# Casting and splitting the value product straight from PSUM in a memory-attention and SwiGLU kernel

## The chip, the cores and the metric

The kernel runs on one core of one Trainium2 chip. The metric is the device time of one execution in microseconds (us), lower is better. Five engines work side by side, each through its own queue in order: TensorE (PE; its weight loads are listed as PEld), VectorE (DVE), ScalarE (ACT), GpSimd (POOL) and SyncE (SP, which issues the DMAs here).

## The reference

Eight batches, eight heads, 576 tokens, head width 64 and 32 memory slots per head; then a SwiGLU block of width 1536 on 4608 rows of 512:

```python
a = softmax(phi, axis=tokens)                    # per head: 576 x 32
k_m = einsum('bhsm,bhsd->bhmd', a, k)            # 32 x 64
v_m = einsum('bhsm,bhsd->bhmd', a, v)
attn = softmax(q @ k_m.T / 8, axis=memory)       # 576 x 32
x = (attn @ v_m), heads side by side             # 4608 x 512
xn = x / sqrt(mean(x * x) + 1e-6) * rms_g
out = (silu(xn @ w_gate) * (xn @ w_val)) @ w_out
```

The weights come as float64, and are converted to float32 on the chip.

## The kernel before, in words

Since `x = attn @ v_m`, the product `xn @ w_gate` equals `attn @ (v_m @ w_gate)` with a scale per row. The kernel never forms `x` for it: it multiplies the small `v_m` of a batch with the weights once (the value product, `vp`), and then multiplies the attention with the result. To keep float32 accuracy, each operand of a product is split into a high part, rounded to the type fp32r, and a low part, what the rounding left; a product is then three matmuls (high x high, high x low, low x high).

A first part, up to about 150 us, makes `k_m`, `v_m` and the attention of the first two pairs of batches. Then comes the part that the change touches: 48 units. A unit `i` belongs to a pair of batches `pr` and a block `j` of 128 columns of the hidden layer; 24 units do the first two pairs of batches over the twelve blocks, 24 more do the other two pairs. A unit consists of these steps:

- `vw_steps(i)`: twelve matmuls (line 852) of the split `v_m` (`vm`) with the split weights (`wh`, `wl`) into `vp`, a PSUM tile of 128 x 1024 float32, two banks, with a single buffer. Its step `evac` (lines 858 to 868) empties it: ScalarE copies the lower 64 partitions into a float32 tile `xf` (line 861), and the upper 64 in two copies that swap the two blocks `b` (line 863); ScalarE casts `xf` to the high part `xh` (line 866); GpSimd subtracts to get the low part `xl` (line 867). `xf` has one buffer, `xh` and `xl` have two each.
- `gv_steps(i)`: in two groups of rows and for both `b`, twelve matmuls (line 889) of `xh`, `xl` with the split attention (`ath`, `atl`) into `pg` and `pv` (two PSUM buffers each); ScalarE takes the silu of `pg` into `sg` (line 897), VectorE multiplies it with `pv` into `hf` (line 898); ScalarE casts `hf` to `hh` (line 911), GpSimd subtracts to get `hl` (line 912).
- `out_steps(i)`, at every second unit: for nine tiles of rows, six matmuls (line 931) of `hh`, `hl` with the split output weights into `po` (two PSUM buffers), and VectorE adds `po` to the sum `acc` in SBUF (line 938; line 936 is the first, a copy). After the last block the sums go out by DMA.

During the first 24 units, VectorE also converts the weights of the coming blocks (`convert`, lines 345 to 385: integer operations on the tiles `ex` and `mi`, then `w`; ScalarE takes a step at line 376), ScalarE casts them (line 402), GpSimd subtracts their low part (`wl` and `ol`, line 403), and the split weights are stored to HBM and read back by the second 24 units. Attention of the last two pairs of batches (`attend_steps`, `x2`: lines 977 to 1021, with tiles `S`, `qT`, `rp`, `at`, which share `po`'s PSUM buffers) is spread over these units too.

The order of the work is written out: each step has a due time, counted in units (`VW`, `GV`, `O`, `PRE` and others in a table `PRM`), the steps are issued in that order, and a scheduler then puts each engine's queue in an order by when it reckons things ready. Every step of the lists `vw_steps(i + 1)` and `gv_steps(i)` is placed so that the value product of the next unit is made while the present one is multiplied.

Of the kernel before, what the change touches and what calls it, by code (L numbers as in the profile page):

```python
# [8 lines left out]
F32 = mybir.dt.float32  # L9
# [4 lines left out]
ALU = mybir.AluOpType  # L14
# [77 lines left out]
def kernel(  # L92
# [24 lines left out]
    nc = tc.nc  # L117
    P = 128
# [309 lines left out]
    with ExitStack() as c1:  # L428
        sb = c1.enter_context(tc.tile_pool(name="sb1", bufs=2, reuse_waits="tile"))
# [394 lines left out]
    sb = ctx.enter_context(tc.tile_pool(name="sb2", bufs=1, reuse_waits="tile"))  # L824
# [5 lines left out]
    def where(i):  # L830

        ps_, r = divmod(i, NU * G * 2)
        u, r = divmod(r, G * 2)
        pi, f = divmod(r, 2)
        return ps_, u, ps_ * G + pi, 2 * u + f

    def vw_steps(i):

        ps_, u, pr, j = where(i)

        def mm(cc):
            def f():
                if cc == 0:
                    vw[i] = [ps.tile([P, 2, 2, 256], F32, tag="vw", name=f"vp{i}", bufs=1)]
                vp = vw[i][0]
                vh, vl = vm[pr][:, 0], vm[pr][:, 1]
                wh, wl = (x.rearrange("p hp g f -> p hp (g f)") for x in wsplit[ps_ * NJ + j])
                for e in range(2):
                    def lhs(vt):
                        return vt[:, cc, e].rearrange("p o x -> p (o x)")  # L850
                    for n, (l, r) in enumerate(((vh, wh), (vh, wl), (vl, wh))):
                        nc.tensor.matmul(  # L852
                            vp[:, cc, e, :], lhs(l), r[:, 2 * cc + e, :],
                            start=(n == 0), stop=(n == 2),
                        )
            return f

        def evac():
            vp = vw[i][0]
            xf = sb.tile([P, 2, 2, 256], F32, tag="xf", name=f"xf{i}")  # L860
            nc.scalar.copy(xf[0:64], vp[0:64])
            for b in range(2):
                nc.scalar.copy(xf[64:128, :, b, :], vp[64:128, :, 1 - b, :])  # L863
            xh = sb.tile([P, 2, 2, 256], F32R, tag="xh", name=f"xh{i}", bufs=2)
            xl = sb.tile([P, 2, 2, 256], F32R, tag="xl", name=f"xl{i}", bufs=2)
            nc.scalar.copy(xh, xf)  # L866
            nc.gpsimd.tensor_tensor(out=xl, in0=xf, in1=xh.bitcast(F32), op=ALU.subtract)  # L867
            vw[i] = xh, xl
        return [mm(0), mm(1), evac]

# [248 lines left out]
```

## Time and profile before

| | |
|---|---|
| median of 3 runs | 942.52 us (942.49 to 943.4) |
| the profiled execution | 941.95 us, of which 940.2 us are the span from the first to the last instruction |
| busy in the span: TensorE | 852.0 us (91%) |
| VectorE | 560.4 us (60%) |
| ScalarE | 433.2 us (46%) |
| GpSimd | 408.7 us (43%) |
| mean granted TensorE clock | 0.962 |
| chain of work that ended last | TensorE 69%, VectorE 20%, DMA 3%, ScalarE 3%, GpSimd 1% |

How to read the rows. A row of a group shows the line of the kernel, the engine, the operation, what it writes and reads, partitions x elements and type, and how many there are; behind the first bar stands the busy time in us and the mean duration of one in ns, behind the second how long the engine stood idle just before such instructions, and what ended that. A row of a single line or tile gives the minimum, median and maximum duration in ns. A row of the waits gives who waited for whom: us in total, times, the longest in us. A row in the order of time gives the start and the duration in us, the instruction, how many were merged, and in square brackets the idle time before it with what ended it. Times count from the first instruction. In the slices of the page each digit is the busy share of a fortieth of the span, in tenths. An engine's idle time is no cost in itself: what counts is the chain of work that ends last.

### The profile page before, as it was taken

To read this page: it belongs to the slowest core of one execution; us is meant where nothing else is said; L and a number is where in the kernel's file an instruction comes from. 1 tells how busy PE (TensorE), PEld (TensorE's weight loads), DVE (VectorE), ACT (ScalarE), POOL (GpSimd) and SP (SyncE) were. 2 spreads that over 40 slices of the span, in tenths; PEclk is the share of its full clock that TensorE was granted. 3 is DMA by queue.
4 is the path that set the end of the run, shared out by engine and by line. 5 is a ranking of instruction groups with operands and counts; after the bars stand their busy time and mean duration, and the time that the engine had idled before them with its cause. 6 is when DMAs were issued, how large, how long until landed. Compare 5 with 4: busy or idle time off the path is not lost.

```text
span 940.2 us, 15899 instructions
## 1 busy us (share of the span) xinstructions
PE 852.0 (91%) x6207; PEld 756.7 (80%) x6207; DVE 560.4 (60%) x998; ACT 433.2 (46%) x743; POOL 408.7 (43%) x290
## 2 busy tenths in 40 slices
PE   5799676689889899897799999999999999999998
PEld 4678565679779688786699898798989999999996
DVE  5487969895897976969843463643333333333333
ACT  2566333656547546465454354343343443443430
POOL 2365636562653554454344354253333423433421
PEclk9889877899899999999899999999999999999999
DMA  8997644452343623434223215341202212030046
GB/s 282 254 288 237 225 134 131 143 159 66 98 158 83 187 76 83 161 100 152 90 64 102 68 60 134 85 115 45 90 1 69 67 36 100 1 129 7 1 107 140
DMA packets 85667, 106.42 MB, mean 113 GB/s; under 512 B 38996, under 2 KB 56920, under 8 KB 85592
## 3 DMA queue, kind: packets, MB, share of 16 engines
q1 hardware_dynamic: 85592, 105.41, 37.7%
q8 instruction: 49, 0.80, 0.4%
q14 instruction: 26, 0.21, 0.1%
HBM read 73.93 MB, written 31.46 MB: 112 GB/s over the span
## 4 chain that ended last, share of the span: by engine, by line
PE 69%; DVE 20%; DMA 3%; issue 3%; ACT 3%; POOL 1%; SPq 0%; DVEq 0%; ACTq 0%; POOLq 0%
PE po L931 28%; PE pv L889 13%; PE pg L889 13%; PE vp L852 5%; DVE mi L369 3%; DVE mi L365 3%; DVE w L385 2%; PE kvp L583 2%; PE xp L235 2%; DVE ex L345 2%; DMA phi<-in_phi_dram 2%; DVE ex L358 1%; DVE acc L938 1%; DVE ex L357 1%; DVE ex L352 1%
## 5 line engine op out<-in xcount | busy, mean ns | idle before, releaser
L912 POOL TENSOR_TENSOR hl<-hf,hh 128x512 fp32r<-128x512 f32 (+1 forms) x96 | 143.6, 1496 | 235.1 <-ACT hh L911 180.6
L938 DVE TENSOR_TENSOR acc<-po,acc 128x512 f32<-128x512 f32 x180 | 123.8, 689 | 165.4 <-PE po L931 165.2
L931 PE MATMUL po<-oh,hh 128*128 128x512 f32 x432 | 174.4, 405 | 14.3 <-DVE acc L938 12.0
L867 POOL TENSOR_TENSOR xl<-xf,xh 128x1024 fp32r<-128x1024 f32 x48 | 118.3, 2465 | 137.4 <-ACT xh L866 73.6
L931 PE MATMUL po<-oh,hl 128*128 128x512 f32 x432 | 172.0, 398 | 0.0
L931 PE MATMUL po<-ol,hh 128*128 128x512 f32 x432 | 171.5, 397 | 0.0
L897 ACT ACTIVATE sg<-pg 128x256 f32<-128x256 f32 x192 | 78.5, 411 | 189.3 <-PE pg L889 175.5
L898 DVE TENSOR_TENSOR hf<-pv,sg 128x256 f32<-128x256 f32 x192 | 85.4, 452 | 106.9 <-PE pv L889 65.2
L931 PEld LDWEIGHTS po<-oh,hh 128*128 128x128 f32 x432 | 81.7, 190 | 30.5 <-DVE acc L938 15.3
L889 PE MATMUL pv<-ath,xh 128*128 128x320 f32 (+1 forms) x384 | 87.2, 306 | 15.6 <-DVE hf L898 15.6
L852 PE MATMUL vp<-wh,vm 128*128 128x256 f32 x384 | 89.0, 297 | 11.1 <-ACT xf L863 10.8
L931 PEld LDWEIGHTS po<-oh,hl 128*128 128x128 f32 x432 | 81.9, 190 | 19.5
L911 ACT CAST hh<-hf 128x512 fp32r<-128x512 f32 (+1 forms) x96 | 64.6, 674 | 70.7 <-DVE hf L898 40.0
L931 PEld LDWEIGHTS po<-ol,hh 128*128 128x128 f32 x432 | 82.0, 190 | 10.9
L889 PE MATMUL pg<-ath,xh 128*128 128x320 f32 (+1 forms) x384 | 87.2, 302 | 1.1 <-ACT sg L897 1.1
L889 PE MATMUL pg<-ath,xl 128*128 128x320 f32 (+1 forms) x384 | 85.7, 298 | 0.0
L889 PE MATMUL pg<-atl,xh 128*128 128x320 f32 (+1 forms) x384 | 85.7, 299 | 0.0
L889 PE MATMUL pv<-atl,xh 128*128 128x320 f32 (+1 forms) x384 | 83.8, 298 | 0.0
L889 PE MATMUL pv<-ath,xl 128*128 128x320 f32 (+1 forms) x384 | 83.7, 296 | 0.0
L889 PEld LDWEIGHTS pv<-ath,xh 128*128 128x128 f32 x384 | 63.6, 193 | 23.0 <-DVE hf L898 18.4
L852 PEld LDWEIGHTS vp<-wh,vm 128*128 128x128 f32 x384 | 68.8, 201 | 14.1 <-ACT xf L863 11.7
L889 PEld LDWEIGHTS pg<-ath,xh 128*128 128x128 f32 x384 | 64.9, 192 | 7.3 <-ACT sg L897 1.5
(133 smaller groups left out, 1522.7 us busy)
## 6 DMA issues: line engine op xcount, KB each, us to landing
kv<-in_k_dram SPq DMA_DIRECT2D x32, 288.0 KB, 6.2
kv<-in_v_dram SPq DMA_DIRECT2D x32, 288.0 KB, 6.2
out_dram<-acc SPq DMA_DIRECT2D x72, 128.0 KB, 2.4
raw<-in_moe_w_gate_dram SPq DMA_DIRECT2D x12, 512.0 KB, 4.1
raw<-in_moe_w_val_dram SPq DMA_DIRECT2D x12, 512.0 KB, 4.1
wd<-wh SPq DMA_DIRECT2D x12, 512.0 KB, 3.5
wd<-wl SPq DMA_DIRECT2D x12, 512.0 KB, 3.3
raw<-in_moe_w_out_dram SPq DMA_DIRECT2D x12, 512.0 KB, 3.6
```

The costliest lines, as they stand in the source:

```text
L235: nc.tensor.matmul(xp[64 * j:64 * j + 64, P * cc:P * cc + P], st["at"][:, t, cc, 64 * j:64 * j + 64], gb[:, j, cc], start=True, stop=True,)
L365: V.tensor_scalar(out=m, in0=d["raw"][:, :, 1], scalar1=0xFFFFF, scalar2=None, op0=ALU.bitwise_and)
L369: V.scalar_tensor_tensor(out=mf, in0=d["raw"].bitcast(U32)[:, :, 0], scalar=2.0 ** -32, in1=m, op0=ALU.mult, op1=ALU.add,)
L852: nc.tensor.matmul(vp[:, cc, e, :], lhs(l), r[:, 2 * cc + e, :], start=(n == 0), stop=(n == 2),)
L867: nc.gpsimd.tensor_tensor(out=xl, in0=xf, in1=xh.bitcast(F32), op=ALU.subtract)
L889: nc.tensor.matmul(pt[:, :N], l[:, cc, b, half * P:half * P + P], r[:, b, cc, t0:t0 + n, :].rearrange("p t x -> p (t x)"), start=(m == 0), ...
L897: nc.scalar.activation(sg[:, :N], pg[:, :N], AF.Silu)
L898: nc.vector.tensor_tensor(out=hf[:, :, b, :], in0=pv[:, :N].rearrange("p (t x) -> p t x", x=64), in1=sg[:, :N].rearrange("p (t x) -> p t x ...
L911: nc.scalar.copy(hh, hv)
L912: nc.gpsimd.tensor_tensor(out=hl, in0=hv, in1=hh.bitcast(F32), op=ALU.subtract)
L931: nc.tensor.matmul(po, l[:, tt, :], r, start=(m == 0), stop=(m == 5))
L938: nc.vector.tensor_tensor(out=accs[key], in0=po, in1=accs[key], op=ALU.add)
```

## The change

ScalarE casts the product straight from PSUM into `xh`, in two instructions of 64 partitions; the upper half reads the two blocks `b` in reverse order. VectorE subtracts `xh` from the same PSUM data into `xl`, again in two halves. The float32 tile `xf`, its three copies, and GpSimd's subtraction are gone. The sizes and buffers of `xh`, `xl` and `vp`, and the due times, are as before.

```diff
         def evac():
             vp = vw[i][0]
-            xf = sb.tile([P, 2, 2, 256], F32, tag="xf", name=f"xf{i}")
-            nc.scalar.copy(xf[0:64], vp[0:64])
-            for b in range(2):
-                nc.scalar.copy(xf[64:128, :, b, :], vp[64:128, :, 1 - b, :])
             xh = sb.tile([P, 2, 2, 256], F32R, tag="xh", name=f"xh{i}", bufs=2)
             xl = sb.tile([P, 2, 2, 256], F32R, tag="xl", name=f"xl{i}", bufs=2)
-            nc.scalar.copy(xh, xf)
-            nc.gpsimd.tensor_tensor(out=xl, in0=xf, in1=xh.bitcast(F32), op=ALU.subtract)
+            for h in range(2):
+                rows = slice(64 * h, 64 * h + 64)
+                src = vp[rows, :, ::-1, :] if h else vp[rows]
+                nc.scalar.copy(xh[rows], src)
+                nc.vector.tensor_tensor(out=xl[rows], in0=src, in1=xh[rows].bitcast(F32), op=ALU.subtract)
             vw[i] = xh, xl
         return [mm(0), mm(1), evac]
```

## The prediction

> **What bounds the kernel now.** I read the page first: the busy line, the slices, and the group of the instruction that the change removes from GpSimd.
>
> ```profile
> PE 852.0 (91%) x6207; PEld 756.7 (80%) x6207; DVE 560.4 (60%) x998; ACT 433.2 (46%) x743; POOL 408.7 (43%) x290
> PE   5799676689889899897799999999999999999998
> DVE  5487969895897976969843463643333333333333
> L867 POOL TENSOR_TENSOR xl<-xf,xh 128x1024 fp32r<-128x1024 f32 x48 | 118.3, 2465 | 137.4 <-ACT xh L866 73.6
> ```
>
> The slices show two stages behind the start. From about 140 to 500 us VectorE is at six to nine tenths and TensorE has holes; from 500 us TensorE is full and VectorE is at three. I put numbers on this with the busy time by windows (columns: PE, PEld, DVE, ACT, POOL); the last line is the sum over five windows of 24 us (from 140, 188, 308, 380 and 428 us) in which VectorE never rests.
>
> ```profile
> 140.00:476.00 336.00, 287.40 (x1944) 255.59 (x1940) 280.63 (x440) 184.72 (x306) 163.39 (x99) 0.94 0.40 120
> 500.00:940.00 440.00, 432.92 (x2690) 387.20 (x2688) 172.70 (x332) 172.22 (x299) 163.09 (x103) 1.00 0.24 70
> sum 120.00, PE 94.78 PEld 82.70 DVE 118.47 ACT 60.48 POOL 65.67; mean PE 18.96 PEld 16.54 DVE 23.69 ACT 12.10 POOL 13.13
> ```
>
> In the first stretch TensorE idles 48.6 us and VectorE 55.4 us; in the five full windows VectorE idles 1.5 us of 120. Then I asked for TensorE's waits, for 140 to 500 us (three rows) and for 500 to 940 us (the last row).
>
> ```profile
> PE pv L889 <- DVE hf L898: 15.2, 11, 3.3
> PE po L931 <- DVE acc L938: 10.9, 6, 4.3
> PE vp L852 <- ACT xf L863: 10.8, 2, 6.1
> ...
> PE po L931 <- DVE acc L938: 1.1, 1, 1.1
> ```
>
> So the first stage is decided where VectorE's queue runs late, and the second by TensorE alone. Last I looked in the order of time at what makes VectorE late. Four rows, GpSimd ahead of VectorE in each pair:
>
> ```profile
> 158.58 2.55 POOL L867 TENSOR_TENSOR xl<-xf,xh 128x1024 fp32r<-128x1024 f32 x1
> 158.82 2.86 DVE L369 SCALAR_TENSOR_TENSOR mi<-raw,mi 128x512 f32<-128x512 uint32 x1
> ...
> 449.09 2.40 POOL L867 TENSOR_TENSOR xl<-xf,xh 128x1024 fp32r<-128x1024 f32 x1 [0.64 <-ACT xh L866]
> 449.26 2.78 DVE L358 SCALAR_TENSOR_TENSOR ex<-raw,ex 128x512 int32<-128x512 int32 x1
> ```
>
> A weight-conversion step of VectorE that starts during xl's subtraction on GpSimd ends only half a microsecond after it: 158.82+2.86 = 161.68 against 158.58+2.55 = 161.13, and 452.04 against 451.49. The first and the last of 15 such pairs before 500 us are shown. Beyond the median of their own line these 15 instructions took 30.7 us, 2.05 each; seven of them, 13.9 us, lie in the five full windows. Instructions that read PSUM are not stretched, as these rows of minimum, median and maximum show (L385 has both inputs in SBUF, L938 one in PSUM):
>
> ```profile
> L385 DVE TENSOR_TENSOR w<-mi,ex x34: 672/692/2871, 94.2 to 494.2; 128x512 f32<-128x512 f32 x34
> L938 DVE TENSOR_TENSOR acc<-po,acc x180: 628/692/693, 285.3 to 935.5; 128x512 f32<-128x512 f32 x180
> L212 DVE TENSOR_TENSOR at<-at,rp 128x1024 f32<-128x1024 f32 x8 | 9.6, 1213 | 1.8 <-PE rp L204 1.8
> ```
>
> **The change part by part.** The sum is made against the profiled execution: 941.95 us with a span of 940.2, which is 0.57 below the median of 942.52.
>
> ScalarE. It loses three copies and a cast per unit, and gains two casts of 64x1024 from PSUM.
>
> ```profile
> L863 ACT COPY xf<-vp x96: 578/582/587, 154.2 to 899.6; 64x512 f32<-64x512 f32 x96
> L861 ACT COPY xf<-vp x48: 989/1007/1012, 153.2 to 898.1; 64x1024 f32<-64x1024 f32 x48
> L866 ACT CAST xh<-xf x48: 1029/1042/1066, 157.1 to 900.5; 128x1024 fp32r<-128x1024 f32 x48
> ```
>
> No row has a cast that reads PSUM with two blocks swapped; the nearest is L861, same partitions, elements and source, 1.007 us (bounds 0.98, two halves of L863 run together, and 1.16, two apart). The first cast takes L861's place, the second that of the two L863, and the 1.04 us of L866 goes: 1.2 us of ScalarE per unit less. What it can give is read from VectorE's waits before 500 us, which hold what GpSimd gives too:
>
> ```profile
> DVE hf L898 <- ACT sg L897: 6.5, 6, 3.3
> DVE hf L898 <- POOL hl L912: 6.1, 7, 1.8
> DVE w L385 <- POOL wl L403: 3.7, 2, 2.1
> ```
>
> I take half of the 6.5, **-3.2** (bounds 0 and -6.5): the evacuation still stands ahead of sg, only its last third goes.
>
> GpSimd. It loses 118.3 of 408.7 us, 29%. Of the 9.8 us that VectorE waits for it I take that share, **-2.8** (bounds 0 and -9.8). The stretching of VectorE is counted below.
>
> VectorE. It gains two subtractions of 64x1024 per unit, input in PSUM. The nearest row is L212, 1024 elements with one input in PSUM, 1.213 us; half the rows cost the same, if L861 and L866 are a guide (64 and 128 partitions, both about 1.0). So 2.43 us per unit; 22 units evacuate between 140 and 500 us: 53.4 us more, 30.7 less, net 22.7 on an engine with 55.4 us idle. Where VectorE has room it hides; where it has none, it lengthens the stage. Seven of the evacuations start in the five full windows: 7 x 2.43 = 17.0, less the 13.9 that goes there: **+3.1**. The bounds are +22.7, all of it on the path, and -13.9, all subtractions hidden.
>
> ```profile
> 335.10 1.28 DVE L938 TENSOR_TENSOR acc<-po,acc 128x512 f32<-128x512 f32 x2
> ```
>
> Here two accumulations together took 1.28 us, 0.10 less than twice 0.69, so neighbours can overlap; I do not count that. The Trainium skill, "VectorE: DVE Perf Modes", section "Two Vector instructions with no wait between them", says that an instruction whose input starts at another quadrant of partitions than the last read from that memory starts only when all earlier ones have finished: by that the subtraction from partition 64 has no overlap, and the term stays; with overlap it would be about 1.4 us smaller.
>
> The new wait. VectorE's queue now holds an instruction that waits for ScalarE's cast, which waits for the value product; behind it stand acc and hf, for which TensorE waits. In the full windows VectorE may reach it up to one cast (1.0 us) early; taken at half in seven units, **+3.5** (bounds 0, and 22 for one cast in each of 22 units).
>
> Release of vp. Its PSUM buffer is single. It is free today after the copies, 1.01+1.07 = 2.08 us from their start, and then after one cast and two subtractions, 3.43. The next product waited directly for it twice (10.8 us, the row above): 2 x 1.35 = **+2.7** (up to 30 if all 22 waited).
>
> The float32 copy as a place to stand. In the middle four of these rows the copy is done 20 us before its cast, which waits for pv's matmuls to finish with xh's two buffers:
>
> ```profile
> 214.03 1.01 ACT L861 COPY xf<-vp 64x1024 f32<-64x1024 f32 x1
> 221.12 1.05 ACT L866 CAST xh<-xf 128x1024 fp32r<-128x1024 f32 x1
> ...
> 309.05 1.06 ACT L863 COPY xf<-vp 64x512 f32<-64x512 f32 x2
> 313.37 0.41 PE L852 MATMUL vp<-wh,vm 128*128 128x256 f32 x1
> ...
> 315.34 0.29 PE L852 MATMUL vp<-wh,vm 128*128 128x256 f32 x1
> 329.80 1.05 ACT L866 CAST xh<-xf 128x1024 fp32r<-128x1024 f32 x1 [1.77 <-PE pv L889]
> ...
> 521.70 1.00 ACT L861 COPY xf<-vp 64x1024 f32<-64x1024 f32 x1
> 538.65 1.05 ACT L866 CAST xh<-xf 128x1024 fp32r<-128x1024 f32 x1
> ```
>
> With the copy, the next product could run at 313 us; without it vp stays full until after 329.8, and 2.26 us of TensorE work (313.37 to 315.63) moves back. In 13 units before 540 us the cast starts over 5 us behind the first copy (the outer rows are the first and the last of them). Postponing costs only when TensorE has nothing else, and it idled 48.6 of 336 us: 13 x 2.26 x 0.145 = **+4.3** (bounds 0 and 29).
>
> The second stage. This unit stands for the regular ones (ScalarE, VectorE, TensorE):
>
> ```profile
> 714.39 1.01 ACT L861 COPY xf<-vp 64x1024 f32<-64x1024 f32 x1 [0.86 <-PE vp L852]
> 715.85 0.69 DVE L938 TENSOR_TENSOR acc<-po,acc 128x512 f32<-128x512 f32 x1 [1.30 <-PE po L931]
> 717.20 0.42 DVE L898 TENSOR_TENSOR hf<-pv,sg 128x256 f32<-128x256 f32 x1 [0.66 <-PE pv L889]
> 719.67 0.39 PE L931 MATMUL po<-oh,hh 128*128 128x512 f32 x1
> ```
>
> The first cast would end at 715.4 and both subtractions by 717.9. The accumulation of 715.85 then ends at 718.6 at the latest; TensorE writes its buffer again at 719.67. It fits, so **0** here; if a reordering took that 1.1 us of cover in all 24 units, a microsecond late in each would be +24.
>
> Sum: 3.1 + 3.5 + 2.7 + 4.3 - 3.2 - 2.8 = +7.6; of the two terms that rest on nothing but a share (new wait, lost copy) I keep their sum at 6 rather than 7.8, as they exclude each other where VectorE is the late one. That leaves +5.8: 947.8 for the profiled execution, 948.3 as a median. I say 948.
>
> **The rivals.** *Faster.* The weight steps are no longer stretched, and the subtractions fall into VectorE's idle time, as it could have done here, where a unit's copies had ended at 300.2 (ScalarE) and VectorE then waited 1.64 us:
>
> ```profile
> 299.16 1.07 ACT L863 COPY xf<-vp 64x512 f32<-64x512 f32 x2
> 302.26 0.69 DVE L385 TENSOR_TENSOR w<-mi,ex 128x512 f32<-128x512 f32 x1 [1.64 <-POOL wl L403]
> ```
>
> Then the full windows give 13.9, and with ScalarE's and GpSimd's shares less 2.7 for vp the change is -17.2: 925; half of it gives 933. For it: ten of TensorE's waits stand directly behind a step stretched by xl, as the 4.3 us for acc does behind the L358 at 449.26. Against it: those stretches are shorter than the two subtractions that replace them. It decides when fewer than 30.7/2.43 = 12.6 of the 22 pairs lie on the path. The Trainium skill, "SBUF — State Buffer", section "Who interferes with whom", has the pair of ports shared by the two engines as an exclusive lock for a whole instruction, and says that a VectorE instruction with at most one SBUF input, outside its two-port modes, does not contend; by that the new subtractions are immune. The trace agrees: L938 has 693 ns at most.
>
> *No change.* What comes and goes on VectorE cancels (+3.1 is close to that), and the postponed products find other work: within 0.2% of 942.5, that is 1.9 us, about what a measurement of this kernel can tell from no change.
>
> *Much slower.* The subtractions hold up acc and hf in every unit of the first stage, as a queue without gaps: half of 53.4 us, with the lost copy on top, is 26.7 + 4.3 = +31: about 973. For it: VectorE at 84% there. Against it: 53.9 of its 55.4 us of idle time lie outside the full windows.
>
> *The change does not do what it says* as to the lock: hl, wl and ol stay on GpSimd and can start earlier, and stretch the same steps. That takes the 13.9 away and leaves the subtractions: +5.8 + 13.9 = +19.7, or 962, inside the slower cases.
>
> **How the numbers follow.** The forecast, slower by 2 to 18 us (944.5 to 960.5), gets 0.38; much slower 0.12; no change 0.14; faster 0.36. So faster 0.36, same 0.14, slower 0.50. Leaving out a tenth at each end gives 929 to 968.
>
> **What would show it.** Right: no VectorE step over 2.4 us beside an xl; two groups of 48 subtractions with a mean of 1.2 us; VectorE near 646 us busy (560.4 + 117 - 31), GpSimd near 290, ScalarE near 375; TensorE's waits before 500 us growing for acc, hf and vp, none after it. Wrong: subtractions of over 1.5 us; TensorE's holes before 500 us shrinking; stretched steps beside hl and wl in place of xl; or a second stage with holes of its own, from an order of the queues that these rows do not show.

## The result, and the profile after

The changed kernel takes 920.68 us (919.53 to 921.27) against 942.5 us; the ratio is 0.9765, with a 95% interval of 0.9748 to 0.9782. It is 21.8 us faster where 5.8 us slower was forecast, and below the low end of the range, 929. The profiled execution took 921.27 us with a span of 919.5, 20.7 us less than the span before.

The page of the changed kernel; its lines after 866 carry numbers one lower than before (the matmul at 889 is now 888, the accumulation at 938 now 937).

```profile
PE 843.9 (92%) x6207; PEld 750.0 (82%) x6207; DVE 633.7 (69%) x1094; ACT 382.2 (42%) x647; POOL 287.7 (31%) x242
PE   4899675799989999999999999999999999999997
DVE  5587969998998978978964664655455454554543
L866 DVE TENSOR_TENSOR xl<-vp,xh 64x1024 fp32r<-64x1024 f32 x96 | 117.0, 1219 | 39.0 <-ACT xh L865 37.6
```

TensorE's row is the one to look at: its holes between the sixth and the twenty-first slice are mostly filled, although VectorE is *busier* than before in the same slices. By windows, the same stretches as before (the second one shifted by the 20 us that were gained):

```profile
140.00:476.00 336.00, 301.13 (x2089) 269.23 (x2086) 304.23 (x498) 172.90 (x286) 120.61 (x89) 0.96 0.40 125
480.00:919.00 439.00, 430.90 (x2663) 385.02 (x2661) 228.42 (x382) 142.89 (x243) 99.01 (x76) 1.00 0.24 71
```

In the first stretch TensorE idles 34.9 us instead of 48.6, with 145 more instructions done; VectorE has 304.2 us of work in it instead of 280.6. In the second stretch TensorE idles 8.1 of 439 us, before 7.1 of 440: nothing was gained or lost there. Unit by unit, the last matmul of `pv` comes 29.4 us sooner at unit 23, and 21.0 to 21.1 us sooner at every unit from 31 to 45.

TensorE's waits from 140 to 480 us after the change:

```profile
PE pg L888 <- ACT xh L865: 8.0, 1, 8.0
PE qtp L976 <- DVE acc L935: 5.7, 3, 2.2
PE pg L888 <- ACT sg L896: 5.0, 4, 2.1
PE pv L888 <- DVE hf L897: 2.2, 3, 1.4
```

pv's waits for hf, 15.2 us before, have shrunk to 2.2, and po's for acc from 10.9 to under 2; transposes that share po's buffers now wait 5.7 us for acc, and the first unit's cast costs 8.0, where vp's two waits of 10.8 us stood before. What makes VectorE late less often shows in the weight steps themselves. Groups from 140 to 500 us, before, with the busy time and the mean behind the bar:

```profile
L385 DVE TENSOR_TENSOR w<-mi,ex 128x512 f32<-128x512 f32 x33 | 35.7, 1081 | 6.0 <-POOL wl L403 3.7 <-POOL ol L403 1.1
L369 DVE SCALAR_TENSOR_TENSOR mi<-raw,mi 128x512 f32<-128x512 uint32 x32 | 35.5, 1110 | 0.0
L358 DVE SCALAR_TENSOR_TENSOR ex<-raw,ex 128x512 int32<-128x512 int32 x32 | 28.3, 885 | 0.3
L365 DVE TENSOR_SCALAR mi<-raw 128x512 int32<-128x512 int32 x32 | 28.0, 874 | 0.0
L345 DVE TENSOR_SCALAR ex<-raw 128x512 int32<-128x512 int32 x32 | 27.9, 872 | 0.4
L357 DVE TENSOR_SCALAR ex<-ex 128x512 int32<-128x512 int32 x32 | 23.7, 740 | 0.0
L352 DVE TENSOR_SCALAR ex<-ex 128x512 int32<-128x512 int32 x32 | 20.7, 648 | 0.0
```

and after:

```profile
L385 DVE TENSOR_TENSOR w<-mi,ex 128x512 f32<-128x512 f32 x33 | 29.6, 896 | 2.3 <-POOL wl L403 0.7 <-POOL ol L403 0.7
L369 DVE SCALAR_TENSOR_TENSOR mi<-raw,mi 128x512 f32<-128x512 uint32 x32 | 28.3, 886 | 0.0
L358 DVE SCALAR_TENSOR_TENSOR ex<-raw,ex 128x512 int32<-128x512 int32 x32 | 24.8, 776 | 0.3
L365 DVE TENSOR_SCALAR mi<-raw 128x512 int32<-128x512 int32 x32 | 21.8, 681 | 0.0
L357 DVE TENSOR_SCALAR ex<-ex 128x512 int32<-128x512 int32 x32 | 20.1, 628 | 0.0
L352 DVE TENSOR_SCALAR ex<-ex 128x512 int32<-128x512 int32 x32 | 19.8, 619 | 0.0
L345 DVE TENSOR_SCALAR ex<-raw 128x512 int32<-128x512 int32 x32 | 18.9, 592 | 0.4
```

The same 225 instructions take 199.8 us before and 163.3 after. This sum is called the weight steps' time below. It is a measure of the stretching of these steps alone, in the profiled execution alone; it does not foretell the time of every kernel that follows.

A second part of the gain is TensorE's own busy time, and there the granted clock plays a part. TensorE was idle 88.2 us of the span before (940.2 - 852.0) and is idle 75.6 now: 12.6 of the 20.7 us. The other 8.1 are its busy time, 852.0 against 843.9 for the same 6207 matmuls. In the kernel before, the hole of 3.27 us ahead of the `pv` matmul at 244.13 was followed by a slow spell. Windows of the kernel before, ahead of it, after it, and after that; the eighth figure, behind POOL's, is the clock:

```profile
236.30:240.80 4.50, 4.50 (x54) 3.66 (x48) 3.85 (x4) 2.22 (x4) 4.41 (x3) 1.00 0.20 41
243.20:250.00 6.80, 5.87 (x22) 5.58 (x23) 6.16 (x12) 5.77 (x9) 2.04 (x2) 0.50 0.20 80
250.00:256.80 6.80, 6.80 (x40) 6.14 (x40) 5.59 (x10) 4.42 (x7) 3.75 (x3) 1.00 0.45 120
```

Between 140 and 700 us the clock stood at half for 41.0 us before and for 27.3 us after; half of the difference, 6.9 us, is near the 8.1. Over the whole span, with the start that the change hardly touches, it is 74.4 us and 68.0, which would give 3.2. So the clock accounts for a part of the 8.1 us; how large a part is not shown. The Trainium skill, "TensorE: Matmul & The Clock Gate", section "Part 1: The HAM clock gate (the "warmup" mystery)", describes a gate that passes half of the pulses after an idle window of about 3.4 us, and all again after a busy window of about that length. The trace agrees on the lengths: between 140 and 700 us the spells last 3.4 us, 6.8 us and once 10.2. It differs on the hole: in the changed kernel one of 2.26 us at 585 us was enough, while in the kernel before one of 2.48 us at 208 us was followed by no spell. So some holes in TensorE's row were paid for more than once.

### The profile page after: what moved, and what is told of

The parts are those of the page before. It is cut to its first block, busy times and chain, and to the rows that moved or that the text cites. A ratio compares the mean times of both kernels' runs of the same rounds, so it can differ in the third digit from the quotient of the medians.

```text
span 919.5 us, 15815 instructions
## 1 busy us (share of the span) xinstructions
PE 843.9 (92%) x6207; PEld 750.0 (82%) x6207; DVE 633.7 (69%) x1094; ACT 382.2 (42%) x647; POOL 287.7 (31%) x242
## 4 chain that ended last, share of the span: by engine, by line
PE 59%; DVE 14%; issue 5%; ACT 3%; POOL 1%; DVEq 0%; ACTq 0%; POOLq 0%
PE po L930 26%; PE pv L888 13%; PE pg L888 13%; PE vp L852 5%; DVE xl L866 2%; DVE mi L369 1%; DVE hf L897 1%; DVE w L385 1%; DVE acc L937 1%; DVE ex L352 1%; DVE ex L345 1%; DVE mi L365 1%; DVE ex L358 1%; DVE ex L357 1%; DVE acc L935 1%
## 5 line engine op out<-in xcount | busy, mean ns | idle before, releaser
L911 POOL TENSOR_TENSOR hl<-hf,hh 128x512 fp32r<-128x512 f32 (+1 forms) x96 | 139.9, 1457 | 441.8 <-ACT hh L910 439.5
L866 DVE TENSOR_TENSOR xl<-vp,xh 64x1024 fp32r<-64x1024 f32 x96 | 117.0, 1219 | 39.0 <-ACT xh L865 37.6
L865 ACT CAST xh<-vp 64x1024 fp32r<-64x1024 f32 x96 | 96.7, 1007 | 68.3 <-PE vp L852 31.3
L852 PE MATMUL vp<-wh,vm 128*128 128x256 f32 x384 | 86.3, 290 | 2.6 <-DVE xl L866 1.6
L888 PE MATMUL pv<-ath,xh 128*128 128x320 f32 (+1 forms) x384 | 85.1, 302 | 2.7 <-DVE hf L897 2.6
L852 PEld LDWEIGHTS vp<-wh,vm 128*128 128x128 f32 x384 | 66.9, 195 | 5.7 <-DVE xl L866 2.0
```

The costliest lines, as they stand in the source:

```text
L852: nc.tensor.matmul(vp[:, cc, e, :], lhs(l), r[:, 2 * cc + e, :], start=(n == 0), stop=(n == 2),)
L865: nc.scalar.copy(xh[rows], src)
L866: nc.vector.tensor_tensor(out=xl[rows], in0=src, in1=xh[rows].bitcast(F32), op=ALU.subtract)
L888: nc.tensor.matmul(pt[:, :N], l[:, cc, b, half * P:half * P + P], r[:, b, cc, t0:t0 + n, :].rearrange("p t x -> p (t x)"), start=(m == 0), ...
L911: nc.gpsimd.tensor_tensor(out=hl, in0=hv, in1=hh.bitcast(F32), op=ALU.subtract)
```

## The experiments

Three theories were set against each other: that GpSimd's subtraction held up VectorE's weight steps (*stretching*), that ScalarE's lighter work gave the gain (*ScalarE*), and that the scheduler happened on a better order (*order*; of the 6207 matmul records of TensorE, at most 4965 stand in a common order in the two traces). Times are compared through each run's ratio to the kernel before, since that one's median differed by up to 2 us between the runs.

### The order: shifted due times, with and without the change

```diff
-    VW=[-0.204, 0.03, 0.165],          # b_v1, n_v1
+    VW=[-0.16, 0.07, 0.2],
-    O=[0.115, 0.297, 0.451, ...],      # b_v4, n_v4
+    O=[0.2, 0.36, 0.451, ...],
```

> The kernel before with the due times of the value product's steps moved later by 0.04, 0.04 and 0.035 units; no other edit. It reorders about a fifth of TensorE's instructions. Stretching: still within 1% of 942.5, since the order matters less than the 30.7 us of stretched steps. Order: it may land anywhere between 920 and 960, as far from 942.5 as the changed kernel.

> The same shift of due times in the changed kernel. Stretching: within 1% of 921, and 15 to 30 us below its twin without the change. Order: the distance to its twin has no fixed sign.

> The kernel before with the first two due times of the output steps moved later by 0.085 and 0.063 units. It reorders about a quarter of TensorE's instructions. Stretching: within 1% of 942.5. Order: anywhere between 920 and 960.

> The same shift of the output steps in the changed kernel. Stretching: within 1% of 921, and 15 to 30 us below its twin without the change. Order: no fixed sign of the distance to its twin.

Measured: 942.88 us without the change (ratio 1.0018, 0.9999 to 1.0037) and 920.91 with it (0.9788, 0.9754 to 0.9821) for the first shift; 946.06 (1.0047, 1.0022 to 1.0072) and 919.12 (0.9779, 0.9752 to 0.9806) for the second. The distance between twins is 2.3% and 2.7%, with the sign of the change, while the neighbours of either kernel lie within half a per cent of it. An accident of the order is unlikely as the cause. It is not ruled out by these runs alone, as the two shifts move less than the change does: 5731 and 5516 of the 6207 records stay in a common order with the kernel before.

### ScalarE's load given back

```diff
+            junk = sb.tile([P, 2, 2, 256], F32, tag="xf", name=f"xf{i}")
+            nc.scalar.copy(junk, xh.bitcast(F32))
```

> The changed kernel with one more ScalarE copy of 128x1024 per unit (xh into a tile nobody reads), 1.04 us, which gives ScalarE most of its old load back. Stretching: 921 to 924 us. ScalarE: 935 to 942. Order: 921.

Measured: 918.75 us, ratio 0.9762 (0.9717 to 0.9807), with 48 more copies of 1.05 us; it is 2 us below what *stretching* and *order* expected, and far from *ScalarE*. This copy stands behind the cast, where nothing waits for it; the old copies stood ahead of it. So ScalarE's load as such costs nothing that shows; the next run has the old copies in their old place.

### The subtraction moved, and nothing else

```diff
-            nc.gpsimd.tensor_tensor(out=xl, in0=xf, in1=xh.bitcast(F32), op=ALU.subtract)
+            nc.vector.tensor_tensor(out=xl, in0=xf, in1=xh.bitcast(F32), op=ALU.subtract)
```

> The kernel before with the float32 copy and all of ScalarE's work kept, and only the subtraction moved from GpSimd to VectorE, as one instruction of 128x1024 out of SBUF. Stretching: 918 to 928 us, VectorE has 1.2 us more per unit but no step beside xl on GpSimd. ScalarE: 940 or more, as nothing of ScalarE's work has gone and VectorE has more. Order: nothing certain, between 920 and 950.

Measured: 917.65 us, ratio 0.9754 (0.971 to 0.9797). With all of ScalarE's copies still there, one word of the code gives the whole gain. The theory of ScalarE falls: no part of its work has gone.

### GpSimd's load given back, in one piece, in bits, and as writes alone

```diff
+            junk = sb.tile([P, 2, 2, 256], F32, tag="xf", name=f"xf{i}")
+            # p_extra (p_extra_r: junk in F32R)
+            nc.gpsimd.tensor_tensor(out=junk, in0=xh.bitcast(F32), in1=xh.bitcast(F32), op=ALU.subtract)
+            # p_tiny instead: ten of 128x8
+            nc.gpsimd.tensor_tensor(out=junk[:, 0, 0, 8 * c:8 * c + 8], in0=s, in1=s, op=ALU.subtract)
+            # p_memset instead: three of these
+            nc.gpsimd.memset(junk, 0.0)
```

> The changed kernel with one more GpSimd subtraction of 128x1024 per unit (xh minus xh, into a tile nobody reads): GpSimd gets its old load back, everything else stays changed. Theory 'stretching' (the 22 us came because VectorE's weight steps are no longer held up behind xl on GpSimd): 935 to 942 us, with 20 to 31 us of stretched VectorE steps beside the new instruction. Theory 'ScalarE' (they came from ScalarE's 1.2 us less per unit and the earlier cast): 921, stretched or not. Theory 'order' (the scheduler happened on a better order of the queues): 921, since 5090 of TensorE's 5345 instructions stand in the order of the changed kernel.

> The changed kernel with ten GpSimd subtractions of 128x8 per unit, tied to xh, into a tile nobody reads: estimated from small GpSimd rows (0.2 us for 128x18), about 2 us of GpSimd per unit, as much as the one subtraction of the first extra-load run (1.9 us, 933.4 us), but in pieces. Stretching (a VectorE step waits for the one GpSimd instruction that runs): 919 to 925 us, no step more than about 0.3 us longer beside them. Rival 'GpSimd's queue' (what costs is that GpSimd is busy and hl, wl and ol come late): 930 to 936 us.

> The changed kernel with one more GpSimd subtraction per unit, now written as fp32r, which makes it as long as the old xl (2.4 us instead of 1.9). Stretching: 936 to 946 us with 15 us or more of stretched steps beside it. If the length of the single GpSimd instruction does not matter: 933 as before.

> The changed kernel with three GpSimd memsets of 128x1024 per unit in a tile nobody reads: GpSimd is busy again, but only writes SBUF. Stretching, if any GpSimd work holds VectorE up: 932 to 942 us. Stretching, if only a GpSimd instruction that reads SBUF holds up VectorE steps with two SBUF inputs (L369, L358, L385), and one that writes still holds up the one-input steps (L345, L365, L352, L357): about half, 925 to 933, with stretched rows of the second kind alone. ScalarE and order: 921.

Measured: `p_extra` 933.36 us, ratio 0.992 (0.9898 to 0.9941), 1.55% above the changed kernel, about 14.6 us; `p_tiny` 924.31, ratio 0.9817 (0.9798 to 0.9836), 0.52% or 4.9 us above it. GpSimd's added rows in `p_extra` and in `p_tiny`:

```profile
L868 POOL TENSOR_TENSOR xf<-xh x48: 1892/1894/3330, 160.1 to 896.2; 128x1024 f32<-128x1024 f32 x48
L870 POOL TENSOR_TENSOR xf<-xh x480: 189/199/1642, 155.9 to 882.4; 128x8 f32<-128x8 f32 x160
```

That is 1.9 us per unit in one piece and about 2.0 us in ten pieces, by the medians. GpSimd is as busy in both; the one piece costs about three times as much, so GpSimd's being busy as such explains at most the smaller part. No VectorE instruction that started during one of the ten pieces took 0.1 us more than its median. The weight steps' time goes from 163.3 us to 177.4 in `p_extra` (+14.1 for +14.6 us of time) and to 168.1 in `p_tiny` (+4.8 for +4.9). This agreement is closer than it deserves: the profiled execution of `p_extra` took 936.45 us, 3 us above its median, and that of `p_tiny` 920.92, the fastest of its four and no longer than the 921.27 of the changed kernel. And the sum does not rank the kernels: it is 171.4 us in `v_copy`, which took 917.65 us, but 166.9 in `v_psum` and 164.6 in `v_halves` below, which took 934.32 and 938.66.

In `p_extra` ten weight steps were stretched beside the new instruction, by 10.2 us in all where 20 to 31 were expected, and its time is below the 935 to 942 of *stretching* as well. The instruction is shorter than xl's 2.4 us was, which may be why. The order is not behind this loss: 5935 of the 6207 records of TensorE stand in a common order with the changed kernel.

`p_extra_r` was meant to try the old length, and did not: its 48 instructions took 1.90 us too. So it is a repeat: 933.11, ratio 0.9904 (0.989 to 0.9919).

`p_memset` took 963.26, ratio 1.0229 (1.0187 to 1.0272), far outside all that was expected. Nothing held the memsets back, so all 144 ran between 153 and 454 us, and GpSimd was busy for 245.8 of the 336 us from 140 on; its time is not comparable. What it does show is which steps are held up. From 140 to 500 us:

```profile
L365 DVE TENSOR_SCALAR mi<-raw 128x512 int32<-128x512 int32 x32 | 37.6, 1174 | 0.0
L352 DVE TENSOR_SCALAR ex<-ex 128x512 int32<-128x512 int32 x32 | 34.0, 1061 | 0.1
L369 DVE SCALAR_TENSOR_TENSOR mi<-raw,mi 128x512 f32<-128x512 uint32 x32 | 29.3, 917 | 0.0
L358 DVE SCALAR_TENSOR_TENSOR ex<-raw,ex 128x512 int32<-128x512 int32 x31 | 25.5, 822 | 0.3
```

The one-input steps L365 and L352 went from 681 and 619 ns in the changed kernel to 1174 and 1061; the two-input steps L369 and L358 from 886 and 776 to 917 and 822 only. Of the other one-input steps, L345 went from 592 to 834, L357 only from 628 to 676. Beside memsets alone no two-input step took more than 0.70 us, while one-input steps took up to 1.27. The Trainium skill, "SBUF — State Buffer", section "Who interferes with whom", has it so: a VectorE instruction with two SBUF inputs contends with a GpSimd one that reads SBUF, not with one that only writes it, while the two-port modes contend with GpSimd. The trace agrees on the two-input steps; that the one-input steps run in a two-port mode is not shown by any row here.

### No subtraction at all, with and without the float32 copy

```diff
-            xl = sb.tile([P, 2, 2, 256], F32R, tag="xl", name=f"xl{i}", bufs=2)
+            xl = xl0                       # zeros, written once
-                nc.vector.tensor_tensor(out=xl[rows], ...)      # no_sub, from the changed kernel
-            nc.gpsimd.tensor_tensor(out=xl, in0=xf, ...)        # b_no_sub, from the kernel before
```

> The changed kernel without the low part's subtraction: xl is a tile of zeros, written once, so no engine subtracts and vp is free after the casts. It prices all that VectorE's 48 pairs of subtractions cost on the path. If they hide as in the rival 'faster': 917 to 921 us. If they cost what the prediction's terms for VectorE, the new wait and vp's release add up to (3.1 + 3.5 + 2.7 = 9.3 us): about 911.

> The kernel before without the low part's subtraction: xl is a tile of zeros, written once; the float32 copy and all of ScalarE's work stay. If GpSimd's subtraction is the whole loss of the kernel before: within 3 us of the changed kernel without subtraction (906.7). If the copy and ScalarE's extra work cost too: 912 to 925.

Measured: `no_sub` 906.7 us, ratio 0.9622 (0.9602 to 0.9641); `b_no_sub` 904.78, ratio 0.9608 (0.9582 to 0.9633). The intervals overlap: without a subtraction, the copy and ScalarE's extra work cost nothing that shows. GpSimd's subtraction alone cost the kernel before 3.9%, 37 us, with 30.4 us of the weight steps' time (199.8 against 169.4). VectorE's 96 subtractions cost the changed kernel 1.4%, 14 us. The difference of the two prices, 23 us, is the change. The 37 us are all that goes with the subtraction: the stretching, GpSimd's time, and waits for xl (TensorE never waited for it directly; ScalarE's copy into the single xf did, 6.1 us in five waits over the whole span). These parts are not separated. Nor is a price one per microsecond of VectorE's work: the 48 subtractions of `v_copy`, half as many, cost 1.5% against `b_no_sub`, as much as the 96.

### As many VectorE instructions, with the copy kept

```diff
+            for h in range(2):
+                rows = slice(64 * h, 64 * h + 64)
+                # v_halves: in0=xf[rows]; v_psum: in0=vp[rows] (blocks reversed for h = 1)
+                nc.vector.tensor_tensor(out=xl[rows], in0=..., in1=xh[rows].bitcast(F32), op=ALU.subtract)
```

> The kernel before with ScalarE's copies and cast kept and the subtraction on VectorE, in two halves of 64 partitions out of SBUF: VectorE has as many and as long instructions as in the changed kernel, and the float32 copy is still there. If the 3 us between the changed kernel (920.7) and the one that only moved the subtraction (917.7) are VectorE's second instruction: 920 to 923 us. If they are the lost float32 copy (the prediction's +4.3): 916 to 918.

> The kernel before with the float32 copy and ScalarE's copies and cast, but VectorE subtracts in two halves out of PSUM, as in the changed kernel. The only difference to the run with 938.7 us is where VectorE reads: no hold-up of the subtraction by GpSimd (12.3 us there before 500 us), and the copy's single buffer no longer waits for VectorE (24.5 us of ScalarE's waits). If these two are the 18 us: 918 to 925. If ScalarE's work is: 935 or more.

Measured: `v_halves` 938.66 us, ratio 0.997 (0.9954 to 0.9986): neither expectation. The second instruction per unit, 1.22 us, cost 2.2% beside `v_copy`, 21 us, more than the 14 us of the whole pair out of PSUM in the changed kernel. Two rows of it point at two possible causes, the subtraction itself (the whole span) and a wait of ScalarE (140 to 500 us):

```profile
L869 DVE TENSOR_TENSOR xl<-xf,xh x96: 1205/1222/2590, 161.4 to 902.9; 64x1024 fp32r<-64x1024 f32 x96
ACT xf L861 <- DVE xl L869: 24.5, 12, 2.9
```

Out of SBUF the subtractions are held up by GpSimd as the weight steps are: the longest took 2.59 us, in the changed kernel 1.23. And the next unit's copy into xf, which has one buffer, stands in ScalarE's queue until VectorE has read the last one.

`v_psum` removes both and keeps the copies: 934.32 us, ratio 0.9923 (0.9905 to 0.9942). The expected 918 to 925 was wrong as well: 4 us came back, not 18. In it vp has both the copies and, later, the cast and the subtractions to wait for, and is released on average 12.5 us after the product in the first 22 units, against 11.4 in the changed kernel; TensorE waits directly for it seven times, 5.4 us. That is not 13.6 us, the distance to the changed kernel. So the two rows explain at most 4 of the 21 us, and why these two kernels are so slow was not settled. ScalarE's copies ahead of the cast may count here; so may the order, as at most 5255 of TensorE's 6207 records stand in a common order in `v_psum` and the changed kernel.

### Going on

```diff
-    CB=0,
+    CB=1,      # L352 becomes max/min on VectorE (L347) and a scale on ScalarE (L350); L357 goes
```

> The kernel that only moves the subtraction to VectorE, and gives ScalarE one step of the later weight conversions: L352 becomes one VectorE step and one ScalarE activation, and L357 goes, so 32 VectorE steps of 0.41 us (before stretching) less and 32 ScalarE activations of about 0.6 us more, before 500 us. If VectorE's load still sets the first stage: 905 to 915 us. If ScalarE's queue becomes late instead: 920 or more.

> The changed kernel with one step of the later weight conversions given to ScalarE, 32 VectorE steps fewer before 500 us. ScalarE has 1.2 us per unit more room than in the kernel that keeps the float32 copy, where the same edit took 917.7 to 914.3. If VectorE's load sets the first stage: 908 to 917. If ScalarE's queue becomes late: 920 or more.

Measured: `v_cb1`, the moved subtraction with this edit, 914.3 us, ratio 0.9707 (0.9688 to 0.9727): inside the expected 905 to 915. Its interval lies wholly below that of the changed kernel, but overlaps that of `v_copy` (0.971 to 0.9797), so the edit's own gain of 3 us is not clear of noise. `n_cb1`, the changed kernel with it, 916.87, ratio 0.974 (0.9718 to 0.9762): inside the expected 908 to 917, but its interval overlaps that of the changed kernel (0.9748 to 0.9782).

## Why the prediction was wrong

**The mechanism was seen, its size was not.** The prediction's rival "faster" named what happened, and gave it 0.36. The step that failed is the term for VectorE: "Where VectorE has room it hides; where it has none, it lengthens the stage", by which only the 13.9 us of stretching in the five full windows counted as relief. With the 2.8 us for GpSimd that makes 16.7 us, where `b_no_sub` shows 37 us for GpSimd's subtraction, beside 30.4 us less of the weight steps' time, in full windows and others. The likely reason is that a stretched step is not work that idle time elsewhere makes good: VectorE is held for two microseconds in the middle of a burst, with acc and hf behind it. TensorE's waits for hf and acc, which the prediction had shown, point that way: pv's and po's were 26.1 us and are 4.1, though 5.7 us of new waits of the transposes came up. That the rival's 925 us came near the 920.7 was in part luck, as two errors offset each other: it let the subtractions hide, which cost 14 us, and it counted less than half of the relief.

**The price of VectorE's new work was nearer, and too high.** Its terms make 17.0 + 3.5 + 2.7 = 23.2 us; `no_sub` gives 14. Duration and count were right: 1.219 us measured for 1.213, 96 of them, and 1.007 us for each cast. GpSimd came to 287.7 us (290 forecast), ScalarE to 382.2 (375), VectorE to 633.7 (646; the steps beside hl, wl and ol were stretched less too, and 6.9 us more of its instructions' durations overlap). No subtraction was held up by GpSimd (1.230 us at most), as the rows that read PSUM had promised.

**The lost float32 copy, +4.3.** The delay came, its cost did not: vp is released 11.4 us after the product, on average of the first 22 units, where it was 8.0 before, but TensorE's direct waits for that went from 10.8 us to 1.5. With that, the +2.7 for the release of vp is not borne out by itself either. `no_sub` and `b_no_sub` show no difference, and the kernels that keep the copy and have as many VectorE instructions are slower, 938.7 and 934.3, not faster; why is open.

**ScalarE, -3.2.** Wrong: nothing shows in `a_extra`, and `v_copy` has the gain with all of ScalarE's work in place. **GpSimd, -2.8**, for coming late, is not contradicted: `p_tiny` shows 4.9 us, its small stretching included.

**The second stage, 0.** Right: the lead of 21 us stays the same to a tenth from unit 31 to 45.

**Not thought of:** the clock. Behind some of TensorE's long holes it stands at half for some microseconds. TensorE's busy time fell by 8.1 us, beside 12.6 us of idle time, and the clock accounts for a part of that.

**The last rival,** that hl, wl and ol would start earlier and stretch the same steps instead, did not come true: over the whole span the stretching beside them was 48.7 us before and 44.3 after.

## What to carry to other kernels

Where a VectorE step now and then takes as long as the GpSimd instruction beside it, price GpSimd's instruction by the stretched time of all those steps, and not by VectorE's busy share: here 30.4 us of it went with 37 us of time. That is a first estimate and no law, as `v_copy` and `v_psum` show. Give GpSimd short instructions or none while VectorE works out of SBUF at its limit. VectorE's extra work out of PSUM was not held up by GpSimd here (1.23 us at most, against 2.59 out of SBUF); but one subtraction of 128 partitions out of SBUF did no worse than two of 64 out of PSUM. When such a change is tried, move the one operation alone first: here one word gave all that the larger edit gave.

## What the runs showed of the hardware that was not expected

- A GpSimd subtraction of 128x1024 took 1.89 us with the same tile as both inputs (written as float32), 1.90 (written as fp32r), and 2.41 us with two tiles, by the medians.
- Two VectorE subtractions of 64 partitions out of SBUF instead of one of 128 took 938.7 us against 917.7 for the whole kernel, 2.2%, for one more instruction of 1.22 us per unit; the same pair out of PSUM, without the copy, took 920.7.
- Half clock for 6.8 us, from the last microsecond of a hole of 3.3 us in TensorE's work on: 22 matmul records in that spell, 40 in the 6.8 us after it.
